# A Mamba-2 scan followed by a PReLU layer on one core: the first token group in 512-token tiles, its second pair earlier, and both weights converted in turn

## The chip, the cores and the metric

The kernel runs on one core of one Trainium2 chip. The metric is the device time of one execution in microseconds (us). Kernels of one call were run in turn on the same chip; the calls fell on different chips, so across calls only the ratios to the kernel before are compared. The granted clock is the mean TensorE clock in the records, as a share of full speed. TensorE is PE, VectorE DVE, ScalarE ACT, GpSimd POOL, and SyncE, which issues most transfers, SP.

## The reference, cut to what matters

```python
# x (4, 8, 768, 32), a (4, 8, 768), B and C (4, 8, 768, 16); the scan in chunks:
L = exp(cum[:, None] - cum[None, :]) * causal        # decays inside a chunk
y_intra = einsum((C @ B.T) * L, x)
y_inter = (C @ state) * exp(cum)
state   = exp(sum(la)) * state + sum_j(decay_from_j * B_j x_j)
# then 3072 tokens x 256 features:
h = x @ w_in                                          # w_in 256 x 2048, 64-bit floats
g = maximum(h, 0) + alpha * minimum(h, 0)
out = g @ w_out                                       # w_out 2048 x 256, 64-bit floats
```

The weights come as 64-bit floats, and the kernel turns their bits into 32-bit floats on the chip, in sixteen pieces of 512 KB (eight for each weight).

Of the kernel before, what the change touches and what calls it, by code (L numbers as in the profile page):

```python
# [22 lines left out]
def kernel(  # L23
# [25 lines left out]
    nc = tc.nc  # L49
# [17 lines left out]
    GT = GC * Q  # L67
    NG = NCH // GC
    NP = NCH // 2
    LAG = 2  # L70
    LATE = 4
    NQ = NF // 2
    NZ = NF // 4
# [27 lines left out]
    def bank(i):  # L101


        return ps_q.tile([P, 512], F32, name="bank", tag=f"q{i}")
# [5 lines left out]
    def ss_tile():  # L110
        if early[0] is None:
            return ps_s.tile([P, 512], F32, name="ss")
        early[0] += 1
        i = early[0] % (3 if ident_p else 4)
        return ps_s.tile([P, 512], F32, name="ss") if i < 2 else bank(i)
# [75 lines left out]
    def load_weights(dst, src, sg):  # L191
        if src.dtype == F32:
            nc.sync.dma_start(out=dst, in_=src)
            return
        raw = wld.tile([P, 2, WQ, 2], U32, name="raw")
        nc.sync.dma_start(out=raw.rearrange("p k w t -> p k (w t)"), in_=src.bitcast(U32))
        raws[id(dst)] = raw
# [30 lines left out]
    def convert(dst, src, sg, halves=(nc.gpsimd,)):  # L228




        d = dst.bitcast(U32)
        if src.dtype == F32:
            for i in range(2 if sg is not None else 0):
                nc.vector.tensor_scalar(out=d[:, i], in0=d[:, i], scalar1=s_out[:, sg + i : sg + i + 1],
                                        scalar2=None, op0=ALU.bitwise_xor)
            return
        r, t, g = parts.pop(id(dst))
        nc.vector.scalar_tensor_tensor(out=r, in0=t, scalar=3, in1=r,  # L240
                                       op0=ALU.logical_shift_left, op1=ALU.bitwise_xor)


        for i, eng in enumerate(halves):
            ks = slice(2 * i // len(halves), 2 * (i + 1) // len(halves))
            eng.tensor_tensor(out=d[:, ks], in0=r[:, ks], in1=g.bitcast(U32)[:, ks], op=ALU.add)
# [57 lines left out]
    def identity_bank():  # L304


        m5_bank.append(bank(3))
        nc.scalar.copy(out=m5_bank[0][:, HT:], in_=ident_h[:, :HT])
        ident_p.append(m5_bank[0][:, HT:])
# [39 lines left out]
    def pair_loads(gp):  # L349

        b, c = divmod(2 * gp, CPB)
        nat, abc, xt, ap = loads["p", gp]

        bn = work.tile([P, 2, H * N], F32, name="bn")
        i, bi = divmod(b, 2)
        pj = prt[i].rearrange("p (b h c) -> p b c h", b=2, h=H)[:, bi, c : c + 2]
        nc.gpsimd.tensor_tensor(
            out=bn.rearrange("p k (h n) -> p k h n", h=H),
            in0=nat[:, 0].rearrange("p k (h n) -> p k h n", h=H),
            in1=pj.unsqueeze(3).to_broadcast([P, 2, H, N]), op=ALU.mult)  # L360
        return bn

    def first_a(ap, eng):

        z = prep.tile([P, 2, Q], F32, name="z")
        eng.tensor_scalar(out=z.rearrange("p k t -> p (k t)"), in0=ap, scalar1=1e-6,
                          scalar2=1.0, op0=ALU.max, op1=ALU.min)
        eng.memset(z[:, :, :1], 0.0)
        return z
# [14 lines left out]
    def pair(gp):  # L384
# [26 lines left out]
        if gp == 0:  # L411
            z = first_a(ap, nc.vector)
            ahead[0] = spread(z, 0)
            ahead[1] = spread(z, 1, bank)
            rows_turn(0, rows_scan(0))
        elif not abc:
            z = loads.pop(("z", gp))
        bn = bns.pop(gp) if gp in bns else pair_loads(gp)

        pf = ap  # L420
# [10 lines left out]
            decays(1)  # L431


        tp = ss_tile()
        for i in range(2):
            for k in range(2):
                nc.tensor.transpose(tp[:, (2 * i + k) * P : (2 * i + k + 1) * P], nat[:, i, k],  # L437
# [107 lines left out]
    def hidden(g, f, t0, nt):  # L545

        if t0 == 0:
            gts[g, f] = gp.tile([P, GT], F32, name="gt")
        if t0 or g or f % 2:
            hp = ps_h.tile([P, GT], F32, name="hp")[:, :nt]  # L550
        else:
            hp = bank(f // 2 % 2)[:, :nt]
        for k in range(KC):
            nc.tensor.matmul(hp, w_in[:, k, f * P : (f + 1) * P], xts[g][:, k, t0 : t0 + nt],  # L554
                             start=(k == 0), stop=(k == KC - 1))
        gt = gts[g, f][:, t0 : t0 + nt]
        nc.scalar.mul(gt, hp, s_alpha[:, f : f + 1])  # L557
        nc.vector.scalar_tensor_tensor(out=gt, in0=hp, scalar=s_mul[:, f : f + 1], in1=gt,  # L558
                                       op0=ALU.mult, op1=ALU.max)
# [225 lines left out]
    def ssm(gp, stages=1):  # L785

        if gp not in pairs:
            pairs[gp] = pair(gp)
        for i in range(stages):
            next(pairs[gp], None)  # L790

    pieces = in_pieces + out_pieces
    for i in range(2):
        load_weights(*pieces[i])
    load_pair(1)
    for i in range(2, 4):
        load_weights(*pieces[i])
    ssm(0)
    loads["z", 1] = first_a(loads["a", 1], nc.gpsimd)
    ssm(0)  # L800
    convert_a(*pieces[0])
    ssm(0, 2)
    convert(*pieces[0], halves=(nc.vector, nc.gpsimd))
    slopes(alpha)
    rows_out(0)
    load_weights(*pieces[4])
    load_second()
    load_weights(*pieces[5])
    convert_a(*pieces[1])
    ssm(0)  # L810
    convert(*pieces[1])
    convert_a(*pieces[2])

    first = {2: (1, 1), 4: (1, 1), 6: (1, 1), 8: (1, 1), 10: (1, 1), 12: (1, 1), 14: (2, 1)}
    second = {0: (2, 1), 1: (2, 1), 2: (2, 1), 3: (2, 1), 5: (2, 1), 6: (3, 1), 7: (3, 1),
              8: (3, 1), 9: (3, 1), 11: (3, 1), 13: (3, 1)}
    def ahead_of(i):
        if i == len(in_pieces) - 2 or i + 1 >= len(pieces):
            return None
        return pieces[i + 2 if i + 2 < len(in_pieces) else i + 1]  # L820

    in_steps = {6: ((0, 0),), 8: ((0, 1),), 10: ((0, 2),), 15: ((0, 3),)}
    for n in range(2):
        for f in range(NF):
            i = (n * NF + f) // 2
            if (n, f) in ((0, 9), (1, 1), (1, 9)):
                load_pair({(0, 9): 2, (1, 1): 3, (1, 9): 4}[n, f])
            if f in (first, second)[n]:
                ssm(*(first, second)[n][f])
            hidden(0, f, n * 2 * Q, 2 * Q)  # L830
            if (n, f) == (0, 13):
                identity_bank()
            if f % 2 == 0:

                if i + 6 < len(pieces):
                    load_weights(*pieces[i + 6])
                if ahead_of(i):
                    convert(*ahead_of(i))
                if ahead_of(i + 1):
                    convert_a(*ahead_of(i + 1))  # L840
            if n and LAG <= f < NF - LATE + LAG:
                output(f - LAG)
            if n and f in in_steps:
                for q0, part in in_steps[f]:
                    weight_sums(wi, in_sums, q0, part)
    early[0] = None
    token_sums(1)
    ssm(2 * GC // 2, 2)
# [17 lines left out]
    for i in range(NZ * (NG - 1)):  # L866
        g, z = divmod(NZ + i, NZ)
        nxt = 2 * g + 2

        def after(j, g=g, z=z, i=i, nxt=nxt):  # L870
            if i and j in places:
                product(*divmod(NZ + i - 1, NZ), places[j])
            if i == 0:
                for f, half in rest.get(j, ()):
                    output(NF - LATE + f, half)
            if (i, j) in ((0, 13), (1, 8)):
                store_first(i)
            for w, sums, q0, part in late_sums.get((i, j), ()):
                weight_sums(w, sums, q0, part)
            if g > 1 and z == 0 and j in (5, 9, 13, 14):  # L880
                if j == 5:
                    comb[0] = combine(g - 1)
                next(comb[0], None)
            if g > 1 and z in (1, 3) and j == 11:
                finish(g - 1, z // 2)
            if nxt + steps.get((z, j), NP) < NP:
                ssm(nxt + steps[z, j])
            if nxt < NP and (z, j) == (3, 7):
                token_sums(g + 1)
            ahead = nxt + {(1, 3): 1, (3, 8): 2}.get((z, j), NP)  # L890
            if ahead < NP:
                if ahead == 6:
                    rows_turn(1, held["pr"])
                bns[ahead] = pair_loads(ahead)

        comb = [None] if i == 0 else comb
        if z == 0 and nxt < NP:
            if nxt == 4:
                load_rows(1)
                held["pr"] = rows_scan(1)  # L900
                rows_out(1)
            load_pair(nxt + 1)
        if z == 2 and nxt + 2 < NP:
            load_pair(nxt + 2)
        quad(g, z, after)
# [31 lines left out]
```

## The kernel before: the parts that the change and the argument touch

The tokens are done in six groups of 512. A group is two **pairs** of 128-token chunks. `pair` is a generator; each `ssm(gp)` runs it to its next `yield`, so a schedule can lay a pair's stages between other work. Its DVE work is the decay scans, the state and the product of the gram (C times B inside a chunk) with the decays; y is the pair's output, which ACT copies to xT, the input of the hidden tiles:

```python
def pair(gp):
    ...
    tp = ss_tile()                       # transposes of B and C by PE; copies bc, cz by ACT
    ...
    yield
    decays(0)                            # DVE scans (pairs 0 and 1: of rows that PE spreads)
    yield
    decays(1)
    dps = ...                            # PE; then the new state on DVE: dps is free after it
    yield
    gram = {r: (ss_tile() if r < small else ps_h.tile(...)) for r in range(4)}   # PE, 16 matmuls
    for i, r in enumerate(...):          # DVE, four products
        nc.vector.tensor_tensor(out=dec[:, :, hs], in0=gram[r], in1=dec[:, :, hs], op=ALU.mult)
        if i % 2:
            yield
    y = ...                              # PE; copied to xT by ACT
```

The first group has no other group beside it. It goes through `w_in` in sixteen tiles of 128 hidden features, for 256 tokens at a time, since pair 0's tokens are ready before pair 1's:

```python
def hidden(g, f, t0, nt):                # one tile for nt tokens: 2 matmuls on PE,
    ...                                  # one multiply on ACT, one maximum on DVE
def output(f): ...                       # its share of the output, 512 tokens, 4 matmuls on PE
                                         # (the trace lists two records for each of these matmuls)

pieces = in_pieces + out_pieces          # all of w_in first
...                                      # pair 0, five stages
for n in range(2):                       # tokens 0 to 255, then 256 to 511
    for f in range(NF):                  # NF = 16
        if f in (first, second)[n]:
            ssm(*(first, second)[n][f])  # n = 0: pair 1; n = 1: pairs 2 and 3
        hidden(0, f, n * 2 * Q, 2 * Q)
        if f % 2 == 0:
            ...                          # load a piece, convert one, begin the next
        if n and LAG <= f < NF - LATE + LAG:
            output(f - LAG)              # only in the second half

for i in range(NZ * (NG - 1)):           # the main loop: groups 1 to 5
    ...
    if z == 0 and nxt < NP:
        if nxt == 4:
            load_rows(1)
            held["pr"] = rows_scan(1)    # row scans of the second half of the batch, on DVE
            rows_out(1)
        load_pair(nxt + 1)
    quad(g, z, after)
```

The banks of PSUM, to which PE writes its results, go two to `ps_s` and two to `ps_h` (one hidden tile each), and four are named; in this stage two of those hold the outputs.

## Time and profile before

| | kernel before |
|---|---|
| median of the runs beside the change | 401.38 us (399.83 to 402.02, 4 runs) |
| span of the profiled run, mean granted clock | 398.2 us, 0.974 |
| busy: PE, DVE, POOL, ACT | 372.7, 241.5, 199.1, 179.5 us |
| pair 0 done, first hidden tile | 18.9 us |
| first transposes of the next group (end of this stage) | 100.24 us |
| from there to the end | 297.96 us |

PE is busy 94% of the span, so time can be won only where it waits or has a slow clock, and that is ahead of 110 us. The waits are the bracketed entries in PE's order of time; the prediction below shows them.

### The profile page before, as it was taken

The numbers are of one execution on the slowest core, as the hardware profiler recorded it, in microseconds if no ns is written. First come the engines' busy times: TensorE is split into PE (matmuls) and PEld (weight loads), VectorE is DVE, ScalarE is ACT, GpSimd is POOL, SyncE is SP. The second block draws the span as 40 slices with busy tenths as digits, with TensorE's granted clock in tenths as the row PEclk, the third lists the DMA queues.
The fourth block names the chain that finished last, engine by engine and source line by source line (L and its number), as shares of the span: only waits on it lengthen the run. The fifth ranks groups of instructions, "written<-read, shape, count | busy, mean of one in ns | idle before, by whom it ended". The sixth has DMA issues, their size and how long they took to land.

```text
span 398.2 us, 6213 instructions
## 1 busy us (share of the span) xinstructions
PE 372.7 (94%) x2233; PEld 302.2 (76%) x2233; DVE 241.5 (61%) x477; ACT 179.5 (45%) x397; POOL 199.1 (50%) x206
## 2 busy tenths in 40 slices
PE   4698749999799999999999999999999999999995
PEld 4475528888578878878878878878878888888884
DVE  6779575483872673773863874855865754454363
ACT  2574624542344535444444535435535524633541
POOL 3566342467656783563464372365381355355512
PEclk9689968999999999999999999999999999999999
DMA  9788996010180790100540640630720100101003
GB/s 194 159 292 190 308 209 121 0 59 0 27 181 2 127 185 8 53 2 0 78 121 2 90 111 1 103 97 2 114 86 1 27 2 7 22 0 28 0 0 80
DMA packets 121878, 30.71 MB, mean 77 GB/s; under 512 B 93736, under 2 KB 117752, under 8 KB 121848
## 3 DMA queue, kind: packets, MB, share of 16 engines
q1 hardware_dynamic: 116872, 29.87, 33.9%
q10 hardware_dynamic: 4976, 0.46, 0.9%
q8 instruction: 17, 0.28, 0.3%
q14 instruction: 13, 0.11, 0.1%
HBM read 26.98 MB, written 3.34 MB: 76 GB/s over the span
## 4 chain that ended last, share of the span: by engine, by line
PE 86%; DVE 8%; ACT 2%; issue 2%; DMA 1%; POOLq 0%; POOL 0%
PE hp L653 32%; PE bank L628 30%; PE bank L567 7%; PE hp L554 4%; PE ss L531 2%; PE ss L508 2%; DVE dec L406 2%; PE ss L524 1%; PE ss L473 1%; DVE dec L513 1%; DVE wr L240 1%; PE hp L508 1%; DVE dec L400 1%; PE ss L437 1%; DVE gt L558 1%
## 5 line engine op out<-in xcount | busy, mean ns | idle before, releaser
L696 POOL TENSOR_TENSOR gt<-gt 128x512 f32<-128x512 f32 x58 | 73.6, 1270 | 25.7 <-DVE gt L638 19.5
L628 PE MATMUL bank<-gt,w_out 128*128 128x256 f32 x320 | 82.4, 381 | 0.0
L638 DVE SCALAR_TENSOR_TENSOR gt<-hp,s_mul,gt 128x256 f32<-128x256 f32 x120 | 52.6, 480 | 41.4 <-ACT gt L636 40.6
L636 ACT ACTIVATE gt<-hp,s_alpha 128x256 f32<-128x256 f32 x120 | 50.2, 469 | 51.2 <-PE hp L653 40.6
L687 POOL TENSOR_TENSOR gt<-gt 128x512 f32<-128x512 f32 x20 | 25.4, 1270 | 92.9 <-DVE gt L638 92.9
L628 PEld LDWEIGHTS bank<-gt,w_out 128*128 128x128 f32 x320 | 60.2, 190 | 10.2 <-issue 2.3
L628 PE MATMUL bank<-gt,ws 128*128 128x256 f32 x240 | 61.4, 379 | 0.0
L628 PEld LDWEIGHTS bank<-gt,ws 128*128 128x128 f32 x240 | 45.1, 190 | 5.8
L406 DVE TENSOR_TENSOR_SCAN dec<-abc,bank 128x256 f32<-128x256 f32 x80 | 48.2, 662 | 0.0
L653 PE MATMUL hp<-xT,w_in 128*128 128x256 f32 x160 | 43.2, 392 | 0.2
L653 PE MATMUL hp<-xs,w_in 128*128 128x256 f32 x160 | 43.1, 392 | 0.1
L672 DVE TENSOR_TENSOR hp<-hp,u 128x512 f32<-128x512 f32 x20 | 14.0, 698 | 47.7 <-ACT u L670 47.7
L653 PE MATMUL hp<-xs,ws 128*128 128x256 f32 x160 | 41.1, 379 | 0.0
L661 ACT COPY m<-hp 128x512 f32<-128x512 f32 x20 | 11.7, 586 | 57.4 <-PE hp L653 57.4
L653 PEld LDWEIGHTS hp<-xT,w_in 128*128 128x128 f32 x160 | 28.7, 189 | 9.2 <-ACT hp L682 4.7
L653 PEld LDWEIGHTS hp<-xs,w_in 128*128 128x128 f32 x160 | 28.3, 189 | 8.9 <-issue 4.4
L653 PEld LDWEIGHTS hp<-xs,ws 128*128 128x128 f32 x160 | 30.3, 190 | 4.3 <-issue 0.2
L567 PE MATMUL bank<-w_out,gt 128*128 128x256 f32 x128 | 31.9, 391 | 0.0
L554 PE MATMUL hp<-xT,w_in 128*128 128x256 f32 x96 | 27.0, 408 | 2.5 <-DVE gt L558 2.5
L567 PEld LDWEIGHTS bank<-w_out,gt 128*128 128x128 f32 x128 | 25.3, 198 | 4.0 <-issue 0.3
L676 DVE TENSOR_TENSOR c<-hp,m 128x512 f32<-128x512 f32 x20 | 13.6, 681 | 19.3 <-PE hp L653 19.3
L558 DVE SCALAR_TENSOR_TENSOR gt<-hp,s_mul,gt 128x256 f32<-128x256 f32 x24 | 11.5, 478 | 21.5 <-ACT gt L557 21.5
(142 smaller groups left out, 561.3 us busy)
## 6 DMA issues: line engine op xcount, KB each, us to landing
abc<-z SPq DMA_DIRECT2D x20, 512.0 KB, 6.0
raw<-in_moe_w_in_dram SPq DMA_DIRECT2D x8, 512.0 KB, 6.5
raw<-in_moe_w_out_dram SPq DMA_DIRECT2D x8, 512.0 KB, 7.4
xt<-in_x_dram SPq DMA_DIRECT2D x24, 128.0 KB, 3.9
out_dram<-o_sb SPq DMA_DIRECT2D x32, 64.0 KB, 1.9
nat<-in_B_dram SPq DMA_DIRECT2D x22, 64.0 KB, 2.6
nat<-in_C_dram SPq DMA_DIRECT2D x22, 64.0 KB, 3.1
ap<-pf SPq DMA_DIRECT2D x11, 128.0 KB
```

The costliest lines, as they stand in the source:

```text
L406: nc.vector.tensor_tensor_scan(out=dv[:, k, hs], data0=abc[k][:, hs], data1=ident_p[0], initial=0.0, op0=ALU.mult, op1=ALU.add)
L554: nc.tensor.matmul(hp, w_in[:, k, f * P : (f + 1) * P], xts[g][:, k, t0 : t0 + nt], start=(k == 0), stop=(k == KC - 1))
L558: nc.vector.scalar_tensor_tensor(out=gt, in0=hp, scalar=s_mul[:, f : f + 1], in1=gt, op0=ALU.mult, op1=ALU.max)
L567: nc.tensor.matmul(pos[0][t // 2][:, t % 2], gt[:, t * Q : (t + 1) * Q], w_out[:, f], start=(f == 0 and t % 2 == 0), stop=(f == NF - 1), s ...
L628: nc.tensor.matmul(ms[g][i][:, h], w, blocks[g, z][n][:, p], start=(q == 0 and h == 0), stop=(q == NQ - 1), skip_group_check=True)
L636: nc.scalar.mul(o[:, p], h[:, p], s_alpha[:, fs[p]])
L638: nc.vector.scalar_tensor_tensor(out=o[:, p], in0=h[:, p], scalar=s_mul[:, fs[p]], in1=o[:, p], op0=ALU.mult, op1=ALU.max)
L653: nc.tensor.matmul(to[:, p], w(2 * z + p), b, start=start and p == 0, stop=True, skip_group_check=True)
L672: nc.vector.tensor_tensor(out=Y, in0=Y, in1=u2, op=ALU.add)
L676: nc.vector.tensor_tensor(out=c22, in0=A, in1=m5, op=ALU.add)
L687: nc.gpsimd.tensor_tensor(out=tc_, in0=g22, in1=g12, op=ALU.subtract)
L696: eng.tensor_tensor(out=o, in0=x0, in1=x1, op=ALU.subtract)
```

## The change

Intent: let DVE, ACT and POOL do the pair's scans and the conversion beside more PE work. Only four tiles are done for 256 tokens; meanwhile pair 1, whose first stages now lie among pair 0's work, is finished. Every later tile is done for 512 tokens at once and has an output step beside it, which needs a piece of `w_out` as early as one of `w_in`: the pieces alternate. The second row scans leave the main loop's start for its second block.

```diff
-    pieces = in_pieces + out_pieces
+    pieces = in_pieces[:2]
+    for i in range(len(out_pieces)):
+        pieces += in_pieces[i + 2 : i + 3] + out_pieces[i : i + 1]
...
     ssm(0)
     convert_a(*pieces[0])
-    ssm(0, 2)
-    convert(*pieces[0], halves=(nc.vector, nc.gpsimd))
     slopes(alpha)
     rows_out(0)
...
+    load_pair(2)
     ssm(0)
-    convert(*pieces[1])
-    convert_a(*pieces[2])
+    ssm(1)
+    ssm(0)
+    convert_next(halves=(nc.vector, nc.gpsimd))
+    ssm(0)
+    ssm(1)
-    (the loop over n and f above)
+    FIRST = 4
+    for f in range(2):
+        hidden(0, f, 0, 2 * Q)
+    convert_next()
+    ssm(1)
+    for f in range(2, FIRST):
+        hidden(0, f, 0, 2 * Q)
+    ssm(1, 2)
+    convert_next()
+    ssm(1)
+    identity_bank()
+    convert_next()
+    for f in range(FIRST):
+        hidden(0, f, 2 * Q, 2 * Q)
+        if f == 1:
+            convert_next()
+    for f in range(FIRST, NF):
+        if f in (5, 10):
+            load_pair(3 + f // 10)
+        ssm(2 if f <= 9 else 3)
+        hidden(0, f, 0, GT)
+        convert_next()
+        output(f - FIRST)
...
+            if (i, j) == (NZ // 4, 11):
+                held["pr"] = rows_scan(1)
+                rows_out(1)
...
                 load_rows(1)
-                held["pr"] = rows_scan(1)
-                rows_out(1)
```

(Cut: pair 1's spread and transposes get PSUM buffers that do not clash with pair 0's; `hidden` picks its bank by another rule; `load_next`, which issues the piece loads, and `convert_next`, which converts the next piece and begins the one after; the weight sums inside the loop.)

More of the change, by code (lines that the diff above doesn't have):

```diff
@@ L69 @@
     NP = NCH // 2
-    LAG = 2
     LATE = 4
@@ L363, in first_a @@
     def first_a(ap, eng):
-        z = prep.tile([P, 2, Q], F32, name="z")
+        z = prep.tile([P, 2, Q], F32, name="z", bufs=2)
         eng.tensor_scalar(out=z.rearrange("p k t -> p (k t)"), in0=ap, scalar1=1e-6,
@@ L417, in pair @@
             z = loads.pop(("z", gp))
+            ahead[0] = spread(z, 0, bank)
         bn = bns.pop(gp) if gp in bns else pair_loads(gp)
@@ L431, in pair @@
             decays(1)
-        tp = ss_tile()
+        tp = ps_h.tile([P, GT], F32, name="hp") if gp == 1 else ss_tile()
         for i in range(2):
@@ L548, in hidden @@
             gts[g, f] = gp.tile([P, GT], F32, name="gt")
-        if t0 or g or f % 2:
+        if nt < GT and t0 == 0 and f >= 2:
+            hp = bank(f % 2)[:, :nt]
+        else:
             hp = ps_h.tile([P, GT], F32, name="hp")[:, :nt]
-        else:
-            hp = bank(f // 2 % 2)[:, :nt]
         for k in range(KC):
@@ L790, in ssm, with load_next, convert_next @@
             next(pairs[gp], None)
-    pieces = in_pieces + out_pieces
-    for i in range(2):
-        load_weights(*pieces[i])
+    pieces = in_pieces[:2]
+    for i in range(len(out_pieces)):
+        pieces += in_pieces[i + 2 : i + 3] + out_pieces[i : i + 1]
+    loaded, done = [0], [0]
+    def load_next(n=1):
+        for p in pieces[loaded[0] : loaded[0] + n]:
+            load_weights(*p)
+        loaded[0] += n
+    def convert_next(**kw):
+        i = done[0]
+        if i < len(pieces):
+            convert(*pieces[i], **kw)
+            if i + 1 < len(pieces):
+                convert_a(*pieces[i + 1])
+            if loaded[0] == i + 6:
+                load_next()
+        done[0] += 1
+    load_next(2)
     load_pair(1)
-    for i in range(2, 4):
-        load_weights(*pieces[i])
+    load_next(2)
     ssm(0)
@@ L801 @@
     convert_a(*pieces[0])
-    ssm(0, 2)
-    convert(*pieces[0], halves=(nc.vector, nc.gpsimd))
     slopes(alpha)
     rows_out(0)
-    load_weights(*pieces[4])
     load_second()
-    load_weights(*pieces[5])
-    convert_a(*pieces[1])
+    load_next(2)
+    load_pair(2)
     ssm(0)
-    convert(*pieces[1])
-    convert_a(*pieces[2])
-    first = {2: (1, 1), 4: (1, 1), 6: (1, 1), 8: (1, 1), 10: (1, 1), 12: (1, 1), 14: (2, 1)}
-    second = {0: (2, 1), 1: (2, 1), 2: (2, 1), 3: (2, 1), 5: (2, 1), 6: (3, 1), 7: (3, 1),
-              8: (3, 1), 9: (3, 1), 11: (3, 1), 13: (3, 1)}
@@ L817, in ahead_of @@
-    def ahead_of(i):
-        if i == len(in_pieces) - 2 or i + 1 >= len(pieces):
-            return None
-        return pieces[i + 2 if i + 2 < len(in_pieces) else i + 1]
-    in_steps = {6: ((0, 0),), 8: ((0, 1),), 10: ((0, 2),), 15: ((0, 3),)}
-    for n in range(2):
-        for f in range(NF):
-            i = (n * NF + f) // 2
-            if (n, f) in ((0, 9), (1, 1), (1, 9)):
-                load_pair({(0, 9): 2, (1, 1): 3, (1, 9): 4}[n, f])
-            if f in (first, second)[n]:
-                ssm(*(first, second)[n][f])
-            hidden(0, f, n * 2 * Q, 2 * Q)
-            if (n, f) == (0, 13):
-                identity_bank()
-            if f % 2 == 0:
-                if i + 6 < len(pieces):
-                    load_weights(*pieces[i + 6])
-                if ahead_of(i):
-                    convert(*ahead_of(i))
-                if ahead_of(i + 1):
-                    convert_a(*ahead_of(i + 1))
-            if n and LAG <= f < NF - LATE + LAG:
-                output(f - LAG)
-            if n and f in in_steps:
-                for q0, part in in_steps[f]:
-                    weight_sums(wi, in_sums, q0, part)
+    ssm(1)
@@ new lines @@
+    ssm(0)
[18 more added lines that the diff above has]
+            convert_next()
+    in_steps = {8: 0, 10: 1, 12: 2, 14: 3}
+    for f in range(FIRST, NF):
[5 more added lines that the diff above has]
+        output(f - FIRST)
+        if f in in_steps:
+            weight_sums(wi, in_sums, 0, in_steps[f])
```

## The prediction

> **What bounds the kernel now.** I read the busy tenths of the page first, then the stretches, then TensorE (PE) in order of time, then VectorE (DVE) at the places where PE waited. From 60 us on PE is full; before that it is neither full nor always at full clock:
>
> ```profile
> PE   4698749999799999999999999999999999999995
> ...
> PEclk9689968999999999999999999999999999999999
> ```
>
> Each digit is 10 us. The change touches only what comes before about 130 us. Three stretches: rest of the first half of the first group (18.9 to 59 us), its second half (to 100.6), first block of the main loop. The first entry after the length is PE's busy time, the entry before the DMA share its granted clock:
>
> ```profile
> 18.90:59.00 40.10, 30.56 (x196) 21.94 (x196) 30.07 (x56) 23.18 (x49) 22.35 (x25) 0.88 0.89 243
> 59.00:100.60 41.60, 41.60 (x262) 34.65 (x260) 21.92 (x41) 17.18 (x37) 22.04 (x24) 0.95 0.23 49
> 100.60:119.30 18.70, 15.88 (x87) 12.36 (x85) 15.68 (x30) 7.61 (x17) 10.36 (x10) 1.00 0.54 111
> ```
>
> So the slack is 40.10 - 30.56 = 9.5 us of idle PE in the first stretch, 2.8 us in the third, and the slow clock. PE in order of time names the waits (in brackets: idle time and who ended it), and what PE costs when nothing waits:
>
> ```profile
> 40.97 0.71 PE L524 MATMUL bank<-cd,sm 64*128 64x128 f32 x8 [1.47 <-DVE dec L513]
> ...
> 50.82 1.13 PE L554 MATMUL hp<-xT,w_in 128*128 128x256 f32 x4 [2.52 <-DVE gt L558]
> ...
> 57.02 0.79 PE L508 MATMUL ss<-cz,bc 32*128 32x256 f32 x1 [4.44 <-DVE state L484]
> ...
> 86.52 1.03 PE L554 MATMUL hp<-xT,w_in 128*128 128x256 f32 x4
> 87.38 1.89 PE L567 MATMUL bank<-w_out,gt 128*128 128x256 f32 x8
> 89.11 1.03 PE L554 MATMUL hp<-xT,w_in 128*128 128x256 f32 x4
> ...
> 109.09 1.13 PE L653 MATMUL hp<-xT,ws 128*128 128x256 f32 x4 [2.81 <-DVE hp L672]
> ```
>
> Starts 86.52, 87.38, 89.11: a hidden tile for 256 tokens takes 0.865 us, an output step for 512 tokens 1.73. The large waits are all for DVE: it does the pair's decay scans, the state and the weight conversion while PE has only 0.865 us per tile to hide them. The 2.81 us wait is caused by the second half's row scans:
>
> ```profile
> 102.52 0.58 DVE L315 TENSOR_SCALAR r<-rows 96x128 f32<-96x128 f32 x1
> 103.05 0.06 DVE L317 MEMSET r<- 96x1 f32 x1
> 103.14 1.50 DVE L319 TENSOR_TENSOR_SCAN pr<-r,ends 96x128 f32<-96x128 f32 x1
> 104.57 1.42 DVE L330 TENSOR_TENSOR_SCAN rpf<-r,zeros 96x128 f32<-96x128 f32 x1
> ```
>
> **What the Trainium skill says.** "TensorE: Matmul & The Clock Gate", What's actually happening: the array falls to half clock after an idle window of about 3.4 us and needs a busy one to come back. The trace agrees: after the 4.44 us wait the granted clock is 0.64, 0.50 and 0.58 in the 4 us slices from 52 to 64 us, so a wait costs more than its length. "GPSIMD Engine Reference", 1. Specifications: its SBUF interfaces are shared with VectorE, with contention for DVE instructions with two SBUF inputs. It agrees: the row scan took 0.42 us at 5.44 with GpSimd (POOL) idle and 1.50 us above, beside POOL adds; the conversion's two-input step (L240) is 0.68 at the median and 1.15 at worst. "PSUM — Partial Sum Buffer", Specifications: 8 banks of 512 fp32 each per partition. The pools here use 2 + 2 + 4, so a 512-token hidden tile fills one of two banks and the next but one waits until DVE has emptied it; the 2.52 us wait above is that kind of wait. "DMA: Bandwidth & Descriptors", Two DMAs through the same engine are not ordered: a dependent DMA must wait for the earlier one's completion. In the trace the queue waits 0.6 us for the row products to land in DRAM before it reads them back.
>
> **The work that stays.** From PE's first hidden tile (18.89) to the next group's first transposes (100.24) is 81.35 us. Needed in it: 32 half tiles x 0.865 = 27.7; 12 outputs x 1.73 = 20.8; pair 1 (transposes 0.44, two spreads 1.09 each, state 0.59, gram 1.28, y 1.44) 5.9; pair 2 (half a state) 3.5; pair 3 3.8. Sum 61.7, so 19.7 us at most are to be had. The change removes no matmul columns, it re-orders.
>
> **Part 1, pair 1 earlier.** Slopes and row products move ahead of pair 0's products, into DVE's 1.60 us idle before 13.53. Pair 1's spread (cold, about 1.7 us) and transposes (0.66) go into PE's idle from 13.4 to 16.16; ScalarE (ACT) takes its copies (0.58 + 0.91) from 16.0 to 17.5, then weight piece 1 (1.2), then pair 0's xT. So the first hidden tile starts at about 19.1, as before (18.89); DVE has done pair 1's first two scans (2.4) by 19.9 instead of 29.5.
>
> Then, at durations of the trace: hidden tiles 0, 1 end at 21.0 if the clock is up by then (it came up at about 22.4 before), else 22.7. DVE converts piece 1 only after their two activation steps, POOL adds 1.31: ready at 24.0 to 25.5. Meanwhile second scans and state, done 26.2 to 27.8. Tiles 2, 3; gram; four products x 0.64 on DVE end at 29.9 to 31.4; y 1.5 and copy 0.7: 32.2 to 33.7. Four second halves x 0.865 with a start of 0.2: the loop begins at 36 to 37.5; I take 37. PE still idles about 1.3 (piece 1) and 2 to 2.5 us (products) here, all shorter than the 4.44.
>
> **Part 2, twelve tiles of 512 tokens, each with an output.** PE per step 2 x 0.865 + 1.73 = 3.46. One DVE prelu of 512 costs about 0.70 (a 512-wide DVE step from PSUM is 0.698) against 2 x 0.478, ACT about 0.65 against 2 x 0.469: 3 us less on each over twelve, none of it on PE's path. DVE per step: 0.70 + conversion 0.756 + 0.484 + a pair's scans, state and products (8 x 0.61 + 0.7 + 4 x 0.64 = 8.1) over six steps = 3.3 us; POOL 0.63 + 1.33 + weight sums and pair work = about 3; ACT about 2.7. PE with a pair's 3.8 over six is 4.1. **PE becomes the bound on average**, with DVE up to 4.7 us in the two steps with scans. Walking those steps, DVE falls about 1.5 us behind and the gram, which needs a bank that the state frees, waits 0.7 to 1.2 us once per pair. Loop: 12 x 3.46 = 41.5, pairs 7.3, eight transitions x 0.1, waits 2.4: 52. End 89, against 100.24: **11 us**.
>
> **Part 3, pieces of both weights in turn.** Sixteen conversions stay, one per step instead of one per two half tiles. Each piece is ready one and a half or more steps before use (out piece 0 at about 34.6, needed at 38.7). Pair 2's loads now go ahead of most weights: about 2.8 MB at the 300 GB/s seen from 24 to 32 us is 9 us from about 20, landing at 30, needed at 38. Loads are hidden.
>
> **Part 4, second row scans to the main loop's second block.** It gives back the 2.81 us, and its 3.5 us meet DVE at about 132.8, where DVE has 1.81 us of slack before the step PE waits for at 138.2 and PE 0.35 after it: about 1.2 us lost. **Net 1.6.**
>
> Sum 11 + 1.6 = 12.6; a walk misses queueing between engines, so I take off about 1: 401.75 - 11.75 = 390.0 us.
>
> **The rivals.** (a) DVE stays the bound in the loop: every step with scans holds PE. For: DVE was full from 28 to 40 us, and two-input steps stretch beside POOL, which is now busier. Against: 3.3 against 4.1 per step. If each scan step cost 1 us more on PE, 4 us go: 394. (b) The short start is serial: tiles 2, 3 wait for piece 1, y for the products, second halves for y, and ACT holds pair 0's xT behind pair 1's copies. If PE then idles over 3.4 us, the clock drops and the loop starts at about 42 and cold: 395 to 396. (c) Loads: pair 2's 1 MB of decay rows blocks the single in-order queue, weights come late. Against: DMA share 0.23 from 59 us on, and only six pieces stand ahead. If so, 3 to 5 us lost. (d) Better: the clock is up by the first tile and the gram does not wait: loop starts at 36, takes 50, ends at 86: 386.
>
> **Range and chances.** Rivals a to c one at a time give 394 to 396, together they leave little; d gives 386. Range 384 to 397. Two per cent is 393.7. Most ways stay below it, one serious rival crosses it: faster 0.77, within 2% 0.21, slower 0.02.
>
> **What would show it.** First hidden tile at about 19 us; twelfth tile loop from 37 to 89 with PE busy there over 95% and clock 1.0; hidden and output steps 3.46 us apart; no wait of 2 us or more after 37; the wait at the main loop's first block gone; a wait of about 1 us some 35 us later. Wrong if the loop starts after 42, if PE waits for DVE in most scan steps, or if PE waits for weights or pair 2's rows.

## The result, and the profile after

| | before | after |
|---|---|---|
| median | 401.38 us | 385.55 us (384.29 to 386.55, 4 runs) |
| ratio, 95% interval | | 0.9609 (0.9563 to 0.9656) |
| span of the profiled run, clock | 398.2 us, 0.974 | 384.5 us, 0.986 |
| first hidden tile | 18.89 us | 19.03 us |
| first 512-token tile | none | 39.61 us |
| first transposes of the next group | 100.24 us | 88.83 us |
| from there to the end | 297.96 us | 295.67 us |

The changed kernel was timed twice more as a yardstick, in later calls: 385.08 us (0.9607) and 386.05 us (0.9636).

The table already splits the gain of the profiled pair: 100.24 - 88.83 = 11.4 us come from the first group, 297.96 - 295.67 = 2.3 us from behind it. By the pages of the two profiles PE is busy for 372.7 us before and 367.0 after, and idle for 25.5 and 17.5: of these 13.7 us, 8.0 are idle time that went, and 5.7 are the same matmul columns in less busy time, with the granted clock up from 0.974 to 0.986.

The busy tenths of the changed kernel, as shown of before: PE and its clock, 40 slices of 9.6 us.

```profile
PE   5768999999999999999999999999999999999995
...
PEclk9896999999999999999999999999999999999999
```

PE is full from the fifth slice on; before, the last dip (a 7) was in the eleventh, at about 105 us. The slow slices are the fourth (0.6) and little else. By stretch (length, then the busy time of PE, weight load, DVE, ACT and POOL; the first of the last three numbers is the clock): from about the first tile to the first wide tile, and the loop of twelve wide tiles.

```profile
18.90:39.60 20.70, 15.69 (x116) 11.60 (x117) 14.07 (x26) 10.70 (x24) 8.54 (x9) 0.84 0.86 240
39.60:88.80 49.20, 49.19 (x268) 31.80 (x269) 35.27 (x61) 26.38 (x49) 32.48 (x35) 1.00 0.67 160
```

In the loop PE is busy for 49.19 of 49.20 us at full clock, while DVE is busy for 35.27: PE is the bound, and all else is hidden. What is left of waiting lies in the 20.70 us ahead of it. PE in order of time, with its waits:

```profile
19.03 1.99 PE L554 MATMUL hp<-xT,w_in 128*128 128x256 f32 x8 [1.35 <-ACT xT L538]
...
24.16 1.99 PE L554 MATMUL bank<-xT,w_in 128*128 128x256 f32 x8 [1.46 <-POOL w_in L245]
...
29.98 0.55 PE L524 MATMUL bank<-cd,sm 64*128 64x128 f32 x1 [2.75 <-DVE dec L513]
...
33.14 5.56 PE L554 MATMUL hp<-xT,w_in 128*128 128x256 f32 x16
38.53 0.60 PE L437 MATMUL ss<-ident,nat 128*128 128x128 f32 x4
39.61 1.96 PE L554 MATMUL hp<-xT,w_in 128*128 128x512 f32 x4 [0.48 <-POOL w_in L245]
41.41 1.89 PE L567 MATMUL bank<-w_out,gt 128*128 128x256 f32 x8
43.13 1.88 PE L554 MATMUL hp<-xT,w_in 128*128 128x512 f32 x4
...
50.68 0.48 PE L508 MATMUL bank<-cz,bc 32*128 32x256 f32 x1
...
125.57 1.13 PE L653 MATMUL hp<-xT,ws 128*128 128x256 f32 x4 [0.87 <-DVE hp L672]
```

The first two tiles start as early as before, now at full clock (1.99 us for both). Tiles 2 and 3 wait for weight piece 1, and y of pair 1 waits 2.75 us for DVE's products. Behind that wait the four second halves take 38.53 - 33.14 = 5.4 us in place of 4 x 0.865 = 3.5: the clock had fallen. From 39.61 on a wide tile and an output follow each other at 3.46 us or a little more. The 4.44 us wait for pair 2's state is gone (its gram starts at 50.68 us without a bracket), and the 2.81 us wait in the main loop has become one of 0.87 us, a block later. DVE has done that state just before the gram, at 50.16 + 0.32 = 50.48 us:

```profile
50.16 0.32 DVE L484 SCALAR_TENSOR_TENSOR state<-state,ap,ss 128x128 f32<-128x128 f32 x1
```

### The profile page after: what moved, and what is told of

Read it like the earlier page. It is cut to its first block, busy times and chain, and to the rows that moved or that the text cites. A ratio compares the mean times of both kernels' runs of the same rounds, so it can differ in the third digit from the quotient of the medians.

```text
span 384.5 us, 6092 instructions
## 1 busy us (share of the span) xinstructions
PE 367.0 (95%) x2185; PEld 290.8 (76%) x2185; DVE 239.7 (62%) x465; ACT 177.4 (46%) x385; POOL 198.6 (52%) x206
## 4 chain that ended last, share of the span: by engine, by line
PE 90%; DVE 4%; ACT 2%; DMA 1%; POOL 1%; issue 1%; POOLq 0%; DVEq 0%; ACTq 0%
PE hp L653 32%; PE bank L628 30%; PE bank L567 7%; PE hp L554 7%; PE ss L531 3%; PE ss L508 2%; PE ss L524 1%; PE ss L473 1%; PE bank L377 1%; PE hp L508 1%; PE bank L508 1%; PE ss L437 1%; DVE dec L405 1%; DMA ap<-in_a_dram 1%; POOL w_in L245 1%
## 5 line engine op out<-in xcount | busy, mean ns | idle before, releaser
L638 DVE SCALAR_TENSOR_TENSOR gt<-hp,s_mul,gt 128x256 f32<-128x256 f32 x120 | 52.5, 479 | 41.3 <-ACT gt L636 40.5
L653 PE MATMUL hp<-xT,w_in 128*128 128x256 f32 x160 | 43.1, 392 | 0.2
L661 ACT COPY m<-hp 128x512 f32<-128x512 f32 x20 | 11.7, 586 | 57.4 <-PE hp L653 52.9
L554 PE MATMUL hp<-xT,w_in 128*128 128x512 f32 (+1 forms) x72 | 30.7, 559 | 2.0 <-ACT xT L538 1.3
L567 PEld LDWEIGHTS bank<-w_out,gt 128*128 128x128 f32 x128 | 24.2, 190 | 8.7 <-issue 6.1
L567 PE MATMUL bank<-w_out,gt 128*128 128x256 f32 x128 | 30.7, 380 | 0.0
L558 DVE SCALAR_TENSOR_TENSOR gt<-hp,s_mul,gt 128x512 f32<-128x512 f32 (+1 forms) x18 | 11.7, 657 | 18.1 <-ACT gt L557 18.1
```

What stands on the lines that cost most here:

```text
L554: nc.tensor.matmul(hp, w_in[:, k, f * P : (f + 1) * P], xts[g][:, k, t0 : t0 + nt], start=(k == 0), stop=(k == KC - 1))
L567: nc.tensor.matmul(pos[0][t // 2][:, t % 2], gt[:, t * Q : (t + 1) * Q], w_out[:, f], start=(f == 0 and t % 2 == 0), stop=(f == NF - 1), s ...
L638: nc.vector.scalar_tensor_tensor(out=o[:, p], in0=h[:, p], scalar=s_mul[:, fs[p]], in1=o[:, p], op0=ALU.mult, op1=ALU.max)
L653: nc.tensor.matmul(to[:, p], w(2 * z + p), b, start=start and p == 0, stop=True, skip_group_check=True)
```

## The experiments

Theory: the gain is one of order. An output beside each tile gives PE 3.46 us of work per step, which hides DVE; moving pair 1 up lets this begin early; the row scans are a small gain of their own. Rivals: the wide instructions unload DVE and ACT; moving pair 1 is the gain by itself; the weights' turn matters in itself. Twelve runs, two of them of the changed kernel itself, were made in three calls, each timed in five rounds, all with correct results. Differences below are of medians in one call, unless a ratio is named.

### The yardsticks: the changed kernel again

> The changed kernel once more, as the yardstick of this call. Expected 0.961 of the kernel before (385.5 us against 401.4), with the loop of twelve 512-token tiles from about 39.6 to 88.8 us and PE idle about 2.7 us near 27 to 30 us, ahead of a slow clock.

Measured: 385.08 us, 0.9607 (0.9577 to 0.9638).

> The changed kernel as yardstick of this call: 0.961 of the kernel before. Its profile should again show a loop start between 37.0 and 39.7 us[...].

Measured: 386.05 us, 0.9636 (0.9604 to 0.9668). The three profiles of this one kernel start their first wide tile at 39.61, 37.05 and 39.10 us: 2.6 us between equal kernels. 1.4 us of it is already there at the first hidden tile (19.03 against 17.62 us; 19.67 in the third); the rest comes behind the 2.75 us wait, where the granted clock differs (see the run with fill matmuls below). A difference of 1 us in where one profile's loop starts is therefore no evidence here; the medians and the waits are.

### The row scans put back, and moved alone

```diff
 # rows_back, on the changed kernel (rows_only: the reverse, on the kernel before)
-            if (i, j) == (NZ // 4, 11):
-                held["pr"] = rows_scan(1)
-                rows_out(1)
...
                 load_rows(1)
+                held["pr"] = rows_scan(1)
+                rows_out(1)
```

> The changed kernel with only the second row scans put back to the start of the main loop. Theory (PE waits where DVE is late, so the place counts): the wait of about 2.8 us before the first block's DVE sum comes back, the 0.9 us wait in the second block goes, so +1.9 us against the changed kernel, and nothing moves before 88 us. Rival (DVE has room there now, since the loop ends with less DVE backlog): under 0.7 us.

Measured: 385.16 us against 385.08, ratio 0.9633 (0.9593 to 0.9673) against 0.9607: +0.1 us by the medians, +1.0 us by the ratios, which the noise does not part. PE in order of time of this kernel:

```profile
93.88 1.13 PE L653 MATMUL hp<-xT,ws 128*128 128x256 f32 x4 [1.60 <-DVE hp L672]
```

The wait came back as 1.60 us, not 2.81, and the later 0.86 us went: 0.7 us net, about the rival's limit. DVE is freer there now: the row scans begin 1.03 us after the next group's transposes (87.39 against 86.36 us), before it was 2.28 us (102.52 against 100.24). The stretch from the next group's first transposes to the end, which is 295.6 to 295.7 us in all three profiles of the changed kernel, takes 382.8 - 86.36 = 296.4 us here: 0.8 us more.

> The kernel before with only the second row scans moved to the main loop's second block. Theory: it gains about 1.9 us by itself (2.81 us wait gone, 0.9 us come back), ratio 0.995. Rival (the scans only move their wait): 0 to 0.5 us, ratio 0.999 to 1.000.

Measured: 398.93 us against 400.81, so 1.9 us faster; ratio 0.9957 (0.9935 to 0.9979), which is 1.7 us. From the next group's first transposes to the end the profile takes 396.3 - 100.61 = 295.7 us, as in the changed kernel, against 297.96 before. On the kernel before the move is worth what the theory says; on the changed kernel, about 0.8 us.

### Wide tiles taken apart

```diff
-        hidden(0, f, 0, GT)
+        hidden(0, f, 0, 2 * Q)
+        hidden(0, f, 2 * Q, 2 * Q)
```

(Also the bank rule of `hidden`, so that the halves use the same two buffers.)

> The changed kernel with every 512-token tile of the loop done as two 256-token tiles back to back: the order stays, only the width of the instructions goes. Theory (PE is the bound in the loop, the gain is one of order): DVE gets 12 x 0.26 = 3 us more and ACT 3 us more, the time moves by less than 1 us. Rival (wide instructions unload DVE and ACT and that is the gain): +3 us or more, with PE waiting for DVE in the two steps with scans of each pair.

Measured: 385.35 us against 385.08, ratio 0.9626 (0.9587 to 0.9664): 0.3 us by the medians, 0.8 by the ratios. The loop takes 87.35 - 37.46 = 49.9 us against 86.26 - 37.05 = 49.2 for the yardstick. The rival asked for 3 us: it falls. The instructions' width is hardly worth anything on time; the order is.

### Pair 1 late in the changed kernel, and early in the kernel before

```diff
 # pair1_late
     ssm(0)
-    ssm(1)
     ssm(0)
     convert_next(halves=(nc.vector, nc.gpsimd))
     ssm(0)
     ssm(1)
     for f in range(2):
         hidden(0, f, 0, 2 * Q)
+    ssm(1)
     convert_next()
```

> The changed kernel with pair 1's first two stages (spread, transposes, copies, first scans) only after pair 0 is done and the first two tiles are issued. Theory (PE's idle time and DVE's gaps before 20 us are what they filled, and the filling keeps PE's clock up): first tiles at half clock, loop starts 4 us later, +3 to +5 us. Rival (the DVE work is the same and is the bound to 30 us anyway): under 1.5 us.

Measured: 393.02 us against 385.08, +7.9 us; ratio 0.9799 (0.9770 to 0.9827). Twice what was expected. PE in order of time of this kernel:

```profile
21.58 1.97 PE L554 MATMUL hp<-xT,w_in 128*128 128x256 f32 x8
...
28.93 3.78 PE L554 MATMUL bank<-xT,w_in 128*128 128x256 f32 x8 [3.69 <-POOL w_in L245]
```

The same of the yardstick of this call:

```profile
17.62 1.99 PE L554 MATMUL hp<-xT,w_in 128*128 128x256 f32 x8 [0.59 <-ACT xT L538]
...
22.76 1.99 PE L554 MATMUL bank<-xT,w_in 128*128 128x256 f32 x8 [1.47 <-POOL w_in L245]
```

The first tile is 3.96 us later than the yardstick's 17.62 (1.9 to 2.6 us later than in the other two profiles of the changed kernel), but not at half clock, as was expected: tiles 0 and 1 take 1.97 us. What the expectation left out is what follows: the scans now stand ahead of piece 1's conversion on DVE, tiles 2 and 3 wait 3.69 us for it in place of 1.47, and then run at half clock (3.78 us for 1.99). The first wide tile comes at 45.95 us against 37.05. So the run does not price pair 1's place alone; it prices it with the conversion behind it.

```diff
 # pair1_early, on the kernel before: pair 1's first two stages among pair 0's
# (cut: slopes and row products move ahead of them, two later stages of pair 1 leave the loop,
#  and the buffers of the spread and the transposes change as in the changed kernel)
     ssm(0)
+    ssm(1)
+    ssm(0)
     convert(*pieces[0], halves=(nc.vector, nc.gpsimd))
     convert_a(*pieces[1])
     ssm(0)
+    ssm(1)
     convert(*pieces[1])
```

> The kernel before with only pair 1 moved up (spread, transposes and first scans among pair 0's work, the row products earlier), its tiles, outputs and weights as they were. Theory (moving pair 1 pays only together with the order behind it: the 2.5 and 4.4 us waits of the kernel before lie at tile 15 and pair 2, which stay): -1 to -3 us, ratio 0.993 to 0.998. Rival (it is the part that carries the gain, as undoing it cost 7.9 us): -7 us or more, ratio under 0.983.

Measured: 399.14 us against 401.00, ratio 0.9950 (0.9921 to 0.9979), so 1.9 us faster. The large waits are still there:

```profile
49.05 1.13 PE L555 MATMUL hp<-xT,w_in 128*128 128x256 f32 x4 [2.12 <-DVE gt L559]
55.25 0.79 PE L509 MATMUL ss<-cz,bc 32*128 32x256 f32 x1 [4.44 <-DVE state L485]
```

In its profile the gain of the first group is larger and in part lost again. The first group ends at 97.18 us against 100.24. But behind the wait in the main loop, 2.84 us against 2.81, the clock is now lower (0.84 and 0.73 in the 4 us slices from 104 to 112 us, 1.00 in both in the kernel before), and from the first group's end to the program's it takes 300.1 us against 297.96.

Moved alone, pair 1 gains 1.9 us; taken out of the change, it costs 7.9. It is a condition of the new order more than a gain of its own.

### The weights in sequence, and the outputs late

```diff
 # pieces_seq has both edits, outputs_late only the second
-    for i in range(len(out_pieces)):
-        pieces += in_pieces[i + 2 : i + 3] + out_pieces[i : i + 1]
+    pieces += in_pieces[2:] + out_pieces
...
-        output(f - FIRST)
+        for o in {12: (4, 5), 13: (6, 7), 14: (8, 9), 15: (10, 11)}.get(f, (f - 8,) if f >= 8 else ()):
+            output(o)
```

> The changed kernel with all pieces of the first weight ahead of all of the second; as the second weight is then late, the loop's outputs start at tile 8 and run two per tile from tile 12, twelve in all as before. Theory (the output beside each tile is what hides DVE): tiles 4 to 7 have PE work of 1.73 us plus pair 2's part against DVE's 3.3 us, so PE waits about 1 us in each, +4 us. Rival (total work is the same and PE catches up later): under 1 us.

Measured: 394.63 us, ratio 0.9836 (0.9802 to 0.9871) against 0.9607 to 0.9636 for the changed kernel: 8 to 9 us lost, twice the expectation.

> The changed kernel with the weight pieces still in turn, but the outputs at the late places of the run with pieces in sequence (first at tile 8, two per tile from 12). Theory (the pieces' turn matters only because it lets an output stand beside each tile, which hides DVE): pair 2's gram waits over 4 us for the state, the clock falls, +6 to +8 us; only the wait of 1.6 us for the second weight is missing of the 9 us. Rival (the order of conversion itself is what counts): under 2 us.

Measured: 394.19 us against 386.05, +8.1 us, ratio 0.9840 (0.9801 to 0.9879). So by the medians the late outputs alone cost as much as both edits. PE in order of time, of pieces_seq and of outputs_late:

```profile
47.80 0.79 PE L508 MATMUL ss<-cz,bc 32*128 32x256 f32 x1 [4.34 <-DVE state L484]
```

```profile
45.42 1.98 PE L554 MATMUL hp<-xT,w_in 128*128 128x512 f32 x4
...
52.38 0.79 PE L508 MATMUL ss<-cz,bc 32*128 32x256 f32 x1 [4.34 <-DVE state L484]
...
54.38 5.56 PE L554 MATMUL hp<-xT,w_in 128*128 128x512 f32 x8
```

This is the wait of the kernel before (4.44 us, DVE's state), back to a tenth. Without the outputs PE runs ahead to pair 2's gram and must wait until DVE has done both scans and the state; the clock falls, and two wide tiles take 5.56 us instead of 3.67. The loop takes 98.85 - 41.45 = 57.4 us against 49.2. The second weight's 1.6 us wait, which was expected to part the two runs, does not show in the medians. It does show in the loop: 96.04 - 36.87 = 59.2 us in pieces_seq, with a wait of 1.61 us for `w_out`, against 57.4. The medians come from two calls, and the starts of equal kernels differ by more than this. The weights' turn pays mainly because it lets the outputs start early.

### PE filled where it waits, and two versions built on it

```diff
 # warm
     ssm(1, 2)
+    fill = ps_h.tile([P, GT], F32, name="hp")
+    for i in range(6):
+        nc.tensor.matmul(fill[:, :WQ], w_in[:, 0, :P], w_in[:, 0, :WQ], start=True, stop=True)
     convert_next()
 # best: also pair 0's y ahead of convert_a of piece 1, and convert_next after the second halves
 # best2: also convert of piece 1 ahead of the first two tiles
```

> The changed kernel with six matmuls on data at hand (2.6 us at full clock, result never read) put where PE waits for the products of pair 1, at 27 to 30 us. Theory (the idle time there costs the clock, and the slow clock costs pair 1's y and the four second halves 1.3 + 1.9 us): granted clock stays 1.0 from 28 to 36 us and the loop starts 3 us earlier, -3 us. Rival (ACT, DVE or conversions bound the loop's start): loop start moves by under 1 us, and PE waits for ACT or POOL in place of the slow clock.

Measured: 384.42 us, ratio 0.9597 (0.9567 to 0.9628). The granted clock in the stretch from 28 to 32 us, after the 2.75 us wait, for the yardstick, for the run with the row scans put back (equal in this stage), and for the filled kernel (the first of the last three numbers is the clock):

```profile
28.00:32.00 4.00, 3.38 (x42) 2.74 (x43) 2.14 (x5) 1.20 (x4) 1.93 (x2) 0.66 0.89 164
```

```profile
28.00:32.00 4.00, 1.73 (x40) 1.37 (x40) 2.81 (x6) 0.69 (x3) 1.32 (x1) 1.00 0.91 139
```

```profile
28.00:32.00 4.00, 4.00 (x36) 3.06 (x28) 3.65 (x7) 1.75 (x4) 0.85 (x2) 1.00 0.99 236
```

The filled kernel keeps the clock, and so do best and best2, which have the filling too (1.00 in each slice from 28 to 40 us). But so does the second one, with the same 2.75 us wait and no filling: it depends on the run. From tile 2 to the first wide tile six profiles with this stage unchanged take 15.45 (the changed kernel at first), 14.29 and 14.30 (yardsticks), 14.31 (split), 14.31 (outputs late) and 12.94 us (row scans back), in the mean 14.27; the filled one takes 12.93. So the clock stayed up in three of three profiles with the filling and in one of six without: this supports the theory's cause without proving it. The expected 3 us was one unlucky profile: against the mean of the six the filling is worth 14.27 - 12.93 = 1.3 us.

> As warm, and pair 0's last copies on ACT go ahead of weight piece 1's, and the conversion inside the second halves goes behind them. Theory: 1 us of PE idle before the first tile and 0.5 us at the loop's start go, so -1 us against warm, -4 us against the changed kernel. Rival: piece 1 is later by as much, so no difference from warm.

Measured: 384.43 us, ratio 0.9589 (0.9565 to 0.9613); no different from warm (384.42). The first tile did start 1.1 us earlier than in warm (19.45 against 20.52) and the first wide tile 1.3 us earlier, but the next group's transposes only 0.3 us (87.47 against 87.80). So the rival had the time right and the reason wrong: piece 1 was not later, as tiles 2 and 3 start 1.1 us earlier too (24.58 against 25.65), but the loop took 50.2 us instead of 49.2.

> As best, and the conversion of weight piece 1 goes ahead of the first two tiles' activation steps on DVE. Theory: tiles 2 and 3 start about 1.4 us earlier and DVE's chain to the products of pair 1 is 0.6 us shorter, so the loop starts about 0.6 us earlier; as the loop then waits for DVE at pair 2's gram, the end moves by 0 to 0.6 us against best. Rival (nothing before the loop counts any more): no difference.

Measured: 384.44 us against 386.05, ratio 0.9598 (0.9570 to 0.9626) against 0.9636. In the same way, a wait appears in the loop:

```profile
48.55 0.48 PE L508 MATMUL ss<-cz,bc 32*128 32x256 f32 x1 [0.27 <-DVE state L484]
```

The first wide tile came at 36.51 us, yet the loop takes 86.68 - 36.51 = 50.2 us here too: what is won ahead of it is partly given back at pair 2's gram, where DVE is now the later one. By the ratios all three versions lie 0.4 to 1.9 us under the changed kernel. The intervals overlap, so that they beat it is likely but not shown.

## Why the prediction was right

The time, 385.55 us, lies in the range of 384 to 397 us, near its low end and 4.5 us under the central 390. Step by step:

- **Part 1, pair 1 earlier: right, but for the clock.** The first tile was to come at 19.1 us; it came at 19.03. That close a hit is luck: the six profiles with this stage unchanged have it from 17.62 to 20.40 us. Its clock was up, the better of the two cases. Piece 1 was to be ready at 24.0 us (tiles 2 and 3 start at 24.16) and the products at 29.9 us (y starts at 29.98). y, copy and second halves were then taken at full clock, giving 36 us for this case; the slow clock after the 2.75 us wait made it 39.61 in the profile, and 37.05 and 39.10 in the yardsticks. The prediction counted a clock loss only behind longer waits (3.4 us in rival b, 4.44 in its trace): that was wrong. It put the waits themselves at 1.3 and 2 to 2.5 us; they were 1.46 and 2.75.
- **Part 2, the loop: right mechanism, term too large.** 52 us were predicted and 49.2 measured. The term that failed is "waits 2.4", the upper end of its own 0.7 to 1.2 us for each of two pairs: pair 2's gram starts at 50.68 us, and DVE has done the state at 50.48, so nothing waits. It was close: in best2, where the loop starts earlier, 0.27 us of that wait appear. DVE's 3.3 us per step were 35.27 / 12 = 2.9.
- The two errors cancel: the loop ends at 88.83 us, predicted 89. This is luck: in the yardstick whose loop starts at the predicted 37 us it ends at 86.26.
- **Part 3, loads hidden: right in effect.** No wait of PE for a transfer shows in the loop. Details were off: the first wide tile waits 0.48 us for the conversion of its piece; the rate read as 300 GB/s is 321 and 392 in the two 4 us slices from 24 to 32 us; and SP waited 4.4 us for the row products to land, against 0.6 before, so pair 2's decay rows were only issued from 28.2 us. They are first used at 43.9.
- **Part 4, the row scans:** 1.6 us net predicted. The profile has 2.81 - 0.87 = 1.9, and 2.3 from the transposes to the end; moved alone they gain 1.9 us. Its own terms for the loss, 3.5 - 1.81 - 0.35, make 1.3 us and not 1.2; the wait that came is 0.87.
- **The deduction of 1 us for queueing** between engines was not needed. Without it the sum is 389. Of the rest, 1.4 us is the starting point: the walk is on a profile of a run of 400.32 us, and was taken off 401.75. With the profiled gain of 13.7 us in place of 12.6, 400.32 gives 386.6, and the profiled run of the changed kernel took 386.52; its median is 1 us lower, within the spread of its runs.
- **Rivals.** That DVE stays the bound in the loop did not come about; both late-output runs show PE waiting for DVE there once the outputs are gone. The slow clock in the short start came as in rival b, without an idle time over 3.4 us, and cost up to 2.5 us instead of 5. Rival c did not occur. Rival d came true by half: clock up at the first tile, no wait at the gram, but no full clock afterwards.

The parts do not add up one by one. Pair 1 alone gains 1.9 us and the row scans alone 1.9; the whole gains 15.8. By subtraction, the remaining 12 us or so belong to the new order of tiles and outputs together with what it needs, and either late outputs or a late pair 1 loses about 8 of them. This remainder is not measured by itself: no run had the wide loop alone on the kernel before, since its outputs need the weights in turn and its tokens need pair 1.

## What to carry to other kernels

When a second engine has as much to do as PE in a stage, give PE its full share of work in every step instead of all light steps first and all heavy ones later: the same sum of work took 8 us less in this loop. Look for what must move so that the heavy step can stand there (a weight piece, an earlier pair), and judge these moves with it, since alone they show little. Before chasing the last microsecond ahead of a PE-bound loop, check that the loop does not hand it back, and profile the same kernel twice.

## What the Trainium skill lacked or had wrong

- "TensorE: Matmul & The Clock Gate", Why this matters for your kernels, advises no PE-idle gaps over about 3 us. Here a gap of 2.75 us was enough: six profiles with the same gap show a lowest granted clock of 0.51, 0.66, 0.62, 0.78, 0.78 and, in one, 1.00 in the 4 us slices from 28 to 36 us. In pair1_early a gap of 2.84 us was followed by 0.84 and 0.73, in the kernel before one of 2.81 us at the same place by 1.00. Here a gap under the limit was a risk, not safe, and equal kernels differed in it.
- The same page, What's actually happening, calls the cost of the start-up ramp under 1% of a span and variable from run to run. This agrees in size: the first hidden tile comes at 17.62 to 20.40 us in the six profiles with this stage unchanged, 2.8 us or 0.7% of 385 us. The page warns against fitting to a count of slow matmuls; it lacks the consequence that one profile per kernel cannot price a change of that size.
